# Where the decay powers of the first four chunks come from, and when those of the others are computed

## The chip, the cores and the metric

The kernel runs on one core of one Trainium2 chip. The metric is the device time of one execution in microseconds (us). The engines are TensorE (PE in the profile, its weight loads PEld), VectorE (DVE), ScalarE (ACT), GpSimd (POOL) and SyncE (SP), which issues the DMAs.

## What is computed

A recurrence over 768 steps, for 4 batches of 8 heads of size 40, and two gated feed-forward layers on its output:

```
for t in range(S):
    y[:, :, t] = einsum('bhd,bhde->bhe', r_t, state)
    Sa = einsum('bhde,bhe->bhd', state, a_t)
    state = state * w_t[:, :, None, :] - einsum('bhd,bhe->bhde', Sa, b_t)
    state = state + einsum('bhd,bhe->bhde', v_t, k_t)
x = y as 3072 rows of 320
x = (silu(x @ w_gate) * (x @ w_val)) @ w_out        # 320 -> 1536 -> 320
x = (sigmoid(x @ w_gate2) * (x @ w_val2)) @ w_out2
```

The decays `w` lie between 0.85 and 0.95. All is float32.

## The kernel before

The 768 steps are cut into 12 chunks of 64. Within a chunk the recurrence is linear algebra: every `a` row is multiplied by the running product of the decays up to its step (`p`), every `k` and `b` row ("keys", `tkb`) by the reciprocal product (`r`), and a triangular system of 64 unknowns per head is inverted. Only the state goes from chunk to chunk. So the chunks' states form a chain, and what is needed for a chunk beside the state can be made ahead.

**Stages.** Stage 1 (0 to 698 us) runs the 12 chunks. Each chunk is written as streams of steps, which `merge` interleaves by hand-given rates: `prep_a` of chunk m+2 (scaling of `a` and keys, transposes `tp` at L345, products `kps` at L407, and bn L416/L417, lq L419), `prep_b` of chunk m+1 (the inverse: `halves` for the chunks 0 to 2, `whole` for the later ones, with a trip through DRAM at L460 and L462; then `hps`, `zps`, `xps`), `chain` of chunk m (`qps`, `ups`, `sps` and the state update L658/L659, in two halves of the heads), `post` (L683, L691, L709, L719), and `extra`: layer 1 of chunk m-1's output for the 1536/128 = 12 blocks of weights that are loaded by then (`used[m]` blocks: 3 for the chunks 0 and 1, 5 next). One block for one chunk is a unit: 16 gate matmuls (`gv`, L929) and its output products (`po`, L947). Stage 2 (698 us to the end) runs as one stream of units what layer 1 has left, and layer 2; its gate matmuls are the tile `g`.

**Weight blocks.** `load_w` brings a block in three pieces. Each piece is one DMA into one of six buffers `raw` (L819), and then goes ScalarE L827, GpSimd L828, VectorE L831, L832, L836, L837, ScalarE L847, GpSimd L849 to L855. Blocks 0 to 2 are loaded beside chunk 0, blocks 3 and 4 in `extra(1)`.

**Powers before.** For chunk 0, `first()` makes `p` and `r` with ten scans each of 64 steps on VectorE (L127), and TensorE turns them into PSUM with 20 small matmuls each (L132; a float32 matmul stands as two records in the trace). For all other chunks `powers(n)` handles a group of four chunks at once, with the 32 heads of each chunk on 32 partitions: a load (L194), two clamps on VectorE (L201), and 28 products over 320 elements for `p` and `r` plus the reciprocal (L198, L217). For group 0 (chunks 1 to 3 are taken from it) most of them run on VectorE, right after chunk 0's scaling; for the groups 1 and 2 all run on GpSimd, beside the chunks 0 to 1 and 1 to 2. The results go to DRAM (`pd`, `rd`, L237) and come back in the layout the chunk needs (`pn` L327, `ld` L318, `pe` L351), and GpSimd multiplies with them (L365 for `a`, L369 for keys). `post` uses `pn` too.

**Order.** After `merge` the framework's scheduler orders each engine's queue. An engine runs its queue in order, and an instruction that waits holds what stands behind it. `behind` fixes one instruction after another on its engine.

## Time and profile before

| what | us |
|---|---|
| median of 3 runs | 1353.06 (1348.85 to 1354.39) |
| the profiled execution | 1346.3 |
| its span, first to last instruction | 1344.6 |
| TensorE busy in the span | 1242.4 (92%) |
| VectorE, ScalarE, GpSimd busy | 758.2, 595.3, 587.3 |

The profile gives the busy time of each engine over a stretch, the order of an engine's instructions in time with the idle time ahead of each and what ended it, and groups of instructions by line. The granted clock is that of TensorE as a share of full speed: 1.00 is 2.4 GHz, 0.5 is 1.2 GHz. The stretches below are cut where the second half of a chunk's state update (L659) ends, to within some us: chunk 0 at 97.1 us, chunk 1 at 171, chunk 2 at 235.6, and so on; from there, a later chunk takes 42 to 45 us in the steady part of stage 1.

### The profile page before, as it was taken

The numbers are of one execution on the slowest core, as the hardware profiler recorded it, in microseconds if no ns is written. First come the engines' busy times: TensorE is split into PE (matmuls) and PEld (weight loads), VectorE is DVE, ScalarE is ACT, GpSimd is POOL, SyncE is SP. The second block draws the span as 40 slices with busy tenths as digits, with TensorE's granted clock in tenths as the row PEclk, the third lists the DMA queues.
The fourth block names the chain that finished last, engine by engine and source line by source line (L and its number), as shares of the span: only waits on it lengthen the run. The fifth ranks groups of instructions, "written<-read, shape, count | busy, mean of one in ns | idle before, by whom it ended". The sixth has DMA issues, their size and how long they took to land.

```text
span 1344.6 us, 34131 instructions
## 1 busy us (share of the span) xinstructions
PE 1242.4 (92%) x13965; PEld 1178.6 (88%) x13965; DVE 758.2 (56%) x1575; ACT 595.3 (44%) x1439; POOL 587.3 (44%) x797
## 2 busy tenths in 40 slices
PE   4487988799999999989899999999999999999996
PEld 4376877698898988878898999999999999999996
DVE  8658676885676778686878888943111111111121
ACT  7464635446455655554443444423333333333331
POOL 5457375422232223345786788832222222222221
PEclk7566858699799999999999999999999999999998
DMA  8843738534424543353355554322000000000000
GB/s 227 202 123 92 157 101 179 132 109 123 127 64 122 142 115 77 84 137 110 108 169 170 185 174 153 100 93 68 22 23 22 22 23 23 23 23 22 11 12 14
DMA packets 164632, 130.44 MB, mean 97 GB/s; under 512 B 110832, under 2 KB 142576, under 8 KB 164080
## 3 DMA queue, kind: packets, MB, share of 16 engines
q1 hardware_dynamic: 164464, 128.15, 33.8%
q8 instruction: 112, 1.84, 0.6%
q14 instruction: 56, 0.46, 0.1%
...
## 4 chain that ended last, share of the span: by engine, by line
PE 68%; DVE 12%; DMA 6%; ACT 5%; POOL 4%; issue 4%; SPq 1%; POOLq 0%; ACTq 0%; DVEq 0%
PE g L929 28%; PE po L947 17%; PE gv L929 8%; PE kps L407 3%; PE tp L345 3%; PE yps L709 2%; PE aps L683 2%; DMA wt<-in_a_w_dram 2%; PE qps L619 1%; DMA xs<-ob 1%; PE ups L637 1%; DVE pr L447 1%; DVE ds L837 1%; POOL wp L198 1%; DMA ld<-rd 1%
## 5 line engine op out<-in xcount | busy, mean ns | idle before, releaser
L929 PE MATMUL g<-x,w 128*128 128x256 f32 x3552 | 491.1, 282 | 4.8 <-DVE g L935 2.6
L929 PEld LDWEIGHTS g<-x,w 128*128 128x128 f32 x3552 | 460.5, 189 | 7.0 <-DVE g L935 3.8
L938 POOL TENSOR_TENSOR hl<-g,hh 128x256 fp32r<-128x256 f32 x288 | 221.2, 769 | 460.1 <-ACT hh L937 422.6
L936 DVE TENSOR_TENSOR g<-g,g 128x256 f32<-128x256 f32 x222 | 93.8, 423 | 307.6 <-PE g L929 297.6
L937 ACT CAST hh<-g 128x256 fp32r<-128x256 f32 x288 | 117.0, 406 | 254.1 <-DVE g L936 231.5
L947 PE MATMUL po<-w,hh 128*128 128x320 f32 x1152 | 223.8, 311 | 1.0 <-ACT hh L937 0.6
L947 PEld LDWEIGHTS po<-w,hh 128*128 128x128 f32 x1152 | 175.3, 189 | 2.3 <-ACT hh L937 1.2
L929 PE MATMUL gv<-x,w 128*128 128x256 f32 x1056 | 154.6, 295 | 5.2 <-ACT x L881 2.4
L929 PEld LDWEIGHTS gv<-x,w 128*128 128x128 f32 x1056 | 137.1, 195 | 10.2 <-ACT x L881 3.9
L947 PE MATMUL po<-w,hl 128*128 128x320 f32 x576 | 141.6, 317 | 1.0 <-POOL hl L938 1.0
L933 ACT ACTIVATE g<-g 128x256 f32<-128x256 f32 x222 | 85.1, 383 | 126.3 <-PE g L929 114.9
L849 POOL TENSOR_TENSOR dt<-dt,w 128x384 f32<-128x384 f32 (+1 forms) x72 | 77.4, 1074 | 65.8 <-ACT w L847 29.6
L947 PEld LDWEIGHTS po<-w,hl 128*128 128x128 f32 x576 | 91.3, 189 | 2.7 <-POOL hl L938 1.5
L419 DVE TENSOR_TENSOR lq<-kps,part 64x256 f32<-64x256 f32 x96 | 40.4, 421 | 89.0 <-ACT bn L417 87.6
L407 PE MATMUL kps<-lq,kbt 104*128 104x128 f32 x384 | 72.1, 348 | 9.8 <-ACT kbt L403 6.0
L447 DVE TENSOR_TENSOR pr<-part,sn 128x4 f32<-128x4 f32 (+4 forms) x135 | 78.1, 578 | 2.8
L407 PEld LDWEIGHTS kps<-lq,kbt 104*128 104x128 f32 x384 | 63.8, 252 | 13.9 <-ACT kbt L403 7.6
L453 DVE TENSOR_REDUCE part<-pr 128x2 f32<-128x4 f32 (+4 forms) x135 | 66.7, 494 | 3.1
L847 ACT CAST w<-dt 128x384 fp32r<-128x384 f32 (+1 forms) x72 | 35.5, 495 | 64.0 <-DVE dt L832 57.0
L837 DVE SCALAR_TENSOR_TENSOR ds<-raw,ds 128x384 f32<-128x384 uint32 (+1 forms) x72 | 61.7, 857 | 1.0
L416 ACT ACTIVATE bn<-kps 32x256 f32<-32x256 f32 x96 | 35.9, 374 | 57.3 <-PE kps L407 35.3
L683 PE MATMUL aps<-rbd,ut 104*128 104x128 f32 x384 | 58.1, 296 | 2.6 <-DVE am L691 2.6
(156 smaller groups left out, 1772.3 us busy)
## 6 DMA issues: line engine op xcount, KB each, us to landing
...
```

The source lines that it names most:

```text
L407: nc.tensor.matmul(kps[:, n].rearrange("p h t -> p (h t)"), lhsT=kbt[0:PW, n, :], rhs=lq[m % 3][0:PW, 4 * g4 + n].rearrange("p h t -> p (h ...
L447: nc.vector.tensor_tensor(out=o, in0=xs[:, 0:kk, None, 0:n].to_broadcast([P, kk, 2, n]), in1=sn[:, None, n : n + 2, 0:n].to_broadcast([P, ...
L453: nc.vector.tensor_reduce(out=xs[:, 0:kk, n : n + 2], in_=o, axis=AX.X, op=ALU.add)
L683: nc.tensor.matmul(aps[:, n, h2], lhsT=ut[0:PW, x, 2 * h2 : 2 * h2 + 2].rearrange("p u s -> p (u s)"), rhs=rbd[0:PW, x, h2].rearrange("p b ...
L837: nc.vector.scalar_tensor_tensor(out=sg.bitcast(F32), in0=lo.bitcast(U32), scalar=2.0**-52, in1=sg.bitcast(F32), op0=ALU.mult, op1=ALU.mult,)
L849: sub(out=tf, in0=tf, in1=w.bitcast(F32), op=ALU.subtract)
L929: nc.tensor.matmul(gv[n], lhsT=p, rhs=q, start=e == 0, stop=e == len(seq) - 1)
L933: nc.scalar.activation(out=g, in_=gv[0], func=AF.Sigmoid)
L936: nc.vector.tensor_tensor(out=g, in0=gv[1], in1=g, op=ALU.mult)
L937: nc.scalar.copy(out=hh, in_=g)
L938: self.heng.tensor_tensor(out=hl, in0=g, in1=hh.bitcast(F32), op=ALU.subtract)
L947: self.nc.tensor.matmul(ops[u], lhsT=p[:, us], rhs=q, start=first and n == 0, stop=last and n == 2)
```

## The change

**Chunks 0 to 3** (`FS = 4`) take their powers from scans over whole rows: ten rows of 66 elements stand behind one another on each partition, and one scan of 660 elements does all (L138; the addend is a tile `one` that holds a 1 at the start of each row, and zeros under the row's data restart the product there). `r` runs backwards with the reciprocal of `p`'s end as its start. TensorE turns the results into PSUM with 20 + 20 matmuls `dtp` (L153; two halves each), VectorE multiplies `a` and keys straight from PSUM (L403, L410), and ScalarE copies `p` to `pn`, which goes once to DRAM (`pq`, L172) and is loaded again by `post` (L337). The ends of the chunk (`pend`) come from one product and one small matmul (L160, L166). Group 0's `powers` and its loads, stores, and GpSimd products (L365, L369) for the chunks 1 to 3 are gone.

**Groups 1 and 2** (`all_powers`) are emitted one after the other beside chunk 0, all on GpSimd; group 1's first clamp stands behind chunk 0's keys on VectorE. Each group still stores to `pd` and `rd`. The group-2 load goes into the buffer `wq` that group 1's stores read.

**Weights.** The blocks 3 and 4 are loaded in `extra(0)` (their buffers `wt` and `wq` are those of the groups' powers), so chunk 1's `extra` has 5 blocks instead of 3: two units of layer 1 move from stage 2 (222 to 220 units) to stage 1. Until `extra(0)`, `load_w` has two `raw` buffers instead of six, since the scans of the chunks 1 to 3 live in the other ones (`raw2` to `raw5`).

```
-        load = nc.sync.dma_start(out=q[rows, 0:C]..., in_=w[32 * ms[0] : ...])
-        if n == 1:
-            behind(load, "pn")
+        nc.sync.dma_start(out=q[rows, 0:C]..., in_=w[32 * ms[0] : ...])
...
-            if n == 1:
-                behind(clamp, ("state", 0))
+            behind(clamp, "keys")
...
+    def all_powers():
+        for n in range(1, len(groups)):
+            yield from powers(n)
...
+    def scan(o, x, js, way):
+        flat = lambda t: t[:, js].rearrange("p j t -> p (j t)")[:, ::way]
+        nc.vector.tensor_tensor_scan(
+            out=flat(o), data0=flat(x), data1=flat(one), initial=0.0, op0=ALU.mult, op1=ALU.add
+        )
...
+    def turn(to, x, half):
+        for b2, hs in enumerate(HALF):
+            sel = ident.rearrange(...)[:, :, b2] if half else ident
+            last = nc.tensor.matmul(to[hs], lhsT=x, rhs=sel, ...)
...
+    def scanned(m):
+        x, p, r = scan_tiles(m)
+        load_w0(m, x)
...
+        def by_p(ps, ds):
+            v = ps.rearrange("p (d n h) -> p n h d", n=8, h=2)
+            nc.vector.tensor_tensor(out=pairs(an)[..., ds], in0=heads(xa)[..., ds], in1=v, op=ALU.mult)
+            nc.scalar.copy(out=heads(pn)[..., ds], in_=v)
+        def by_r(ps, ds):
+            v = ps.rearrange("p (d n h) -> p n h d", n=16, h=2)
+            for q in range(2):
+                nc.vector.tensor_tensor(out=pairs(tkb[m % 3], sl)[..., ds], in0=heads(xk[q])[..., ds], in1=v[:, sl], op=ALU.mult)
+        scan_p(x, p)
...
+        scan(r, x, slice(0, 10), -1)
...
-    for _ in powers(0):
-        pass
...
-                todo.append((powers(1), *QP))
+                todo.append((all_powers(), *QP))
...
-                ffn = Ffn(nc, ident, (raws, x_p, h_p, ptp, [(pg, "gv")], po), True)
+                ffn = Ffn(nc, ident, (raws[:2], x_p, h_p, ptp, [(pg, "gv")], po), True)
...
+                if m == 0:
+                    ffn.raw = raws
...
-                for f in {-2: range(NFA - 2), 1: range(NFA - 2, NFA)}.get(m, ()):
+                for f in {-2: range(NFA - 2), 0: range(NFA - 2, NFA)}.get(m, ()):
```

How the queues change, at three places. In the rows, `out<-in` are the program's names; `part_...` are slices of shared buffers.

VectorE, about chunk 0's state updates (`sps` added at L658, decayed at L659), before; `am`, `sn` and `ysb` belong to `post` and to chunk 1's inverse, `wp` and `wq` are group 1's clamps:

```order
L691 TENSOR_TENSOR am<-aps,part_86 128x512 [waits PE_49]
L477 SCALAR_TENSOR_TENSOR sn<-sn,part_86 128x256 [waits Activation_49]
L658 TENSOR_TENSOR part_86<-sps,part_86 40x4x2x40 [waits PE_49]
L658 TENSOR_TENSOR part_86<-sps,part_86 40x4x2x40
L483 TENSOR_TENSOR sn<-sn 128x128 [waits DVE_49]
L659 TENSOR_TENSOR part_86<-part_86,pend 104x4x2x40 [waits DVE_49]
L201 TENSOR_SCALAR wp<-wq 128x2560 [waits DMAHW5_49,DMAHW6_49,DMAHW3_49,DMAHW0_49]
L484 TENSOR_TENSOR sn<-sn 128x8x16 [waits DVE_49,Activation_49]
L831 TENSOR_SCALAR dt<-dt 128x320 [waits Pool_49]
L201 TENSOR_SCALAR wq<-wq 128x2560 [waits DMAHW6_49,DMAHW5_49,DVE_49]
```

After (L716 and L717 are the state updates, L231 the clamps, now of group 2, L483 the products `lq` of chunk 1):

```order
L716 TENSOR_TENSOR part_86<-sps,part_86 40x4x2x40 [waits PE_49]
L716 TENSOR_TENSOR part_86<-sps,part_86 40x4x2x40
L483 TENSOR_TENSOR lq_210<-kps,part_86 64x4x64 [waits Activation_49]
L717 TENSOR_TENSOR part_86<-part_86,pend 104x4x2x40 [waits DVE_49]
L231 TENSOR_SCALAR wp<-wq 128x2560 [waits DMAHW5_49,DMAHW6_49,DMAHW4_49,DMAHW3_49]
L483 TENSOR_TENSOR lq_210<-kps,part_86 64x4x64 [waits PE_49,Activation_49]
L749 TENSOR_TENSOR am<-aps,part_86 128x512 [waits PE_49]
L878 TENSOR_SCALAR dt<-dt 128x384 [waits Pool_49]
L231 TENSOR_SCALAR wq<-wq 128x2560 [waits DMAHW3_49,DMAHW2_49,DMAHW4_49,DMAHW1_49,DVE_49]
L879 SCALAR_TENSOR_TENSOR dt<-raw,dt 128x384 [waits DMAHW5_49,DVE_49]
L483 TENSOR_TENSOR lq_210<-kps,part_86 64x4x64 [waits Activation_49]
L539 STREAM_TRANSPOSE sn<-bn 128x512
```

Before, the clamps of group 1 stand behind the second half of chunk 0's state; now those of group 2 stand behind its first half.

SyncE's queue ahead of the load of chunk 1's values (`v`, `part<-in_a_v`), before; `pn` and `ld` bring powers of chunk 1 or 2 from DRAM, `raw` are weights:

```order
L327 DMA pn<-pd 64x640 x2
L318 DMA ld<-rd 64x2x320 x2
L311 DMA ld<-in_a_a_dram 128x640
L819 DMA raw<-in_w_dram 128x640
L315 DMA ld<-in_a_kb_dram 128x640
L318 DMA ld<-rd 64x2x320 x2
L819 DMA raw<-in_w_dram 128x768 x2
L335 DMA part_203<-in_a_v_dram 64x640 x2
```

After (`pd` and `rd` are stores of group 1, `wq<-in_a_w` is the load of group 2):

```order
L866 DMA raw<-in_w_dram 128x768
L258 DMA pd<-wp 32x65x40 x4
L866 DMA raw<-in_w_dram 128x640
L866 DMA raw<-in_w_dram 128x768
L258 DMA rd<-wq 32x64x40 x4
L866 DMA raw<-in_w_dram 128x768
L226 DMA wq<-in_a_w_dram 128x2560
L866 DMA raw<-in_w_dram 128x640
L346 DMA part_197<-in_a_v_dram 64x640 x2
```

Two groups of four stores and the load of group 2 now stand ahead of the values, and the loads from `pd` and `rd` are gone.

TensorE in the inverse of chunk 1 (`hps`, `zps`, `xps`), up to chunk 1's first `ups`, before; the `kps` are chunk 2's, then chunk 3's:

```order
L524 MATMUL hps<-part_218,pr 16x16 x64
L345 MATMUL tp<-ident,part_88 104x128 x4
L354 MATMUL pep<-ident,part_86 104x16
L407 MATMUL kps<-lq_217,kbt 128x128 x4
L564 MATMUL zps<-x1t,bn 32x32 x32
L345 MATMUL tp<-ident,tkb_89 104x128 x8
L580 MATMUL xps<-part_218,zt 32x32 x32
L407 MATMUL kps<-lq_198,kbt 128x128 x4
L875 MATMUL xtp<-ident,ysb 128x128 x4
L637 MATMUL ups<-qs,part_218 64x40 x15
```

After (`dtp` are the turns of chunk 3's `p`, s_1606, and `r`, s_1607):

```order
L586 MATMUL hps<-part_212,pr 16x16 x64
L153 MATMUL dtp<-ident,s_1606 64x64 x13
L471 MATMUL kps<-lq_211,kbt 128x128 x4
L153 MATMUL dtp<-ident,s_1606 64x64 x3
L626 MATMUL zps<-x1t,bn 32x32 x32
L153 MATMUL dtp<-ident,s_1607 64x128 x15
L471 MATMUL kps<-lq_211,kbt 128x128 x4
L642 MATMUL xps<-part_212,zt 32x32 x32
L153 MATMUL dtp<-ident,s_1607 64x128 x5
L153 MATMUL dtp<-ident,s_1606 64x64 x4
L166 MATMUL dtp<-part_86 104x16
L695 MATMUL ups<-qs,part_212 64x40 x16
```

Chunk 3's 40 turns now stand between the products of chunk 1's inverse, ahead of its `ups`.

## Rows read from the trace of the kernel before

**Rows 1.** Stretches: start:end, length, then busy us (instructions) per engine, clock, DMA, GB/s

```profile
16.00:97.10 81.10, 51.10 (x772) 44.44 (x772) 52.23 (x109) 42.56 (x103) 41.80 (x55) 0.56 0.65 168
97.10:171.00 73.90, 62.82 (x1020) 55.21 (x1016) 54.00 (x94) 38.77 (x92) 43.43 (x52) 0.72 0.53 132
171.00:235.60 64.60, 54.66 (x835) 48.94 (x829) 44.52 (x82) 28.73 (x68) 46.48 (x57) 0.69 0.56 129
235.60:285.90 50.30, 42.49 (x592) 37.76 (x590) 41.29 (x90) 25.35 (x62) 18.05 (x25) 0.80 0.49 134
285.90:333.60 47.70, 45.77 (x672) 41.62 (x673) 31.74 (x65) 26.80 (x65) 11.92 (x16) 0.96 0.41 113
333.60:383.40 49.80, 47.92 (x659) 43.33 (x657) 31.42 (x64) 25.07 (x61) 11.69 (x16) 0.86 0.37 101
...
427.00:470.00 43.00, 43.00 (x654) 39.05 (x654) 33.52 (x74) 25.84 (x63) 12.61 (x17) 1.00 0.46 118
...
700.00:1344.00 644.00, 627.58 (x4952) 623.91 (x4950) 257.58 (x551) 223.89 (x572) 271.15 (x373) 0.99 0.20 64
```

**Rows 2.** VectorE by operation, 0 to 40 us: names, shapes, count | busy, mean ns | idle

```profile
L198 DVE TENSOR_TENSOR wp<-wp 128x320 f32<-128x320 f32 x14 | 10.7, 764 | 0.3
L198 DVE TENSOR_TENSOR wq<-wq 128x320 f32<-128x320 f32 x7 | 3.4, 483 | 0.1
...
L127 DVE TENSOR_TENSOR_SCAN r<-w,r,part 128x63 f32<-128x63 f32 x10 | 2.5, 324 | 0.0
L127 DVE TENSOR_TENSOR_SCAN p<-w,part 128x64 f32<-128x64 f32 x10 | 1.9, 270 | 0.0
...
L156 DVE TENSOR_TENSOR tkb<-tkb,f 128x320 f32<-128x320 f32 x4 | 1.7, 483 | 0.0
```

**Rows 3.** ScalarE in order of time, 36 to 97 us: start, us, operation [idle before]

```profile
58.54 0.54 ACT L827 ACTIVATE dt<-raw 128x384 f32<-128x384 f32 x1 [5.15 <-POOL w L853]
...
70.07 0.49 ACT L827 ACTIVATE dt<-raw 128x320 f32<-128x320 f32 x1 [3.04 <-POOL w L853]
...
80.84 0.55 ACT L827 ACTIVATE dt<-raw 128x384 f32<-128x384 f32 x1 [3.68 <-POOL w L855]
```

**Rows 4.** GpSimd by operation, 97 to 147 us

```profile
L198 POOL TENSOR_TENSOR wp<-wp 128x320 f32<-128x320 f32 x14 | 12.5, 894 | 0.4
```

**Rows 5.** SyncE's DMA queue in order of time, 0 to 260 us

```profile
150.54 7.23 SPq L237 DMA_DIRECT2D rd<-wq  x4
...
209.96 9.32 SPq L237 DMA_DIRECT2D rd<-wq  x4
...
221.51 2.08 SPq L460 DMA_DIRECT2D xd<-part  x2
```

**Rows 6.** VectorE in order of time, 36 to 210 us

```profile
85.92 0.47 DVE L659 TENSOR_TENSOR part<-part,pend 104x320 f32<-104x320 f32 x1
...
107.43 5.12 DVE L490 TENSOR_TENSOR pr<-x,sn 128x128 f32<-128x128 f32 x1
...
172.80 1.50 DVE L201 TENSOR_SCALAR wp<-wq 128x2560 f32<-128x2560 f32 x1 [1.84 <-DMA xs<-ob]
...
207.94 0.70 DVE L457 STREAM_TRANSPOSE x1t<-part 128x512 f32<-128x512 f32 x1
```

**Rows 7.** TensorE in order of time, 0 to 60 us and about 114 us

```profile
5.08 2.40 PE L132 MATMUL f<-ident,p 128*64 128x64 f32 x40 [5.08 <-DVE p L127]
7.26 3.52 PE L132 MATMUL f<-ident,r 128*64 128x128 f32 x40
...
114.10 1.94 PE L709 MATMUL yps<-part,rbd 104*64 104x40 f32 x32 [5.78 <-DVE am L691]
```

**Rows 8.** TensorE, the gate matmuls of stage 2: count, duration, first and last

```profile
L929 PE MATMUL g<-x,w x3552: 274/281/389, 698.1 to 1329.9; 128*128 128x256 f32 x198
```

**Rows 9.** VectorE by operation, 214 to 262 us

```profile
L837 DVE SCALAR_TENSOR_TENSOR ds<-raw,ds 128x384 f32<-128x384 uint32 (+1 forms) x5 | 3.8, 769 | 0.1
...
L832 DVE SCALAR_TENSOR_TENSOR dt<-raw,dt 128x384 int32<-128x384 int32 (+1 forms) x5 | 3.2, 644 | 0.0
```

More of the change, by code (lines that the diff above doesn't have):

```diff
@@ new lines, in scan_p @@
+    def scan_p(x, p):
+        for c in (0, C + 1):
+            nc.vector.memset(x[:, :, c : c + 1], 0.0)
+        xw = x[:, :, 1 : C + 1]
+        nc.vector.tensor_scalar(out=xw, in0=xw, scalar1=WLOW, scalar2=WHIGH, op0=ALU.max, op1=ALU.min)
+        scan(p, x, slice(0, 10), 1)
+        nc.vector.reciprocal(out=one[:, :, C + 1], in_=p[:, :, C])
+    def turn(to, x, half):
+        for b2, hs in enumerate(HALF):
+            sel = ident.rearrange("p (y b h) -> p y b h", b=2, h=2)[:, :, b2] if half else ident
+            last = nc.tensor.matmul(to[hs], lhsT=x, rhs=sel, start=True, stop=True, tile_position=(0, hs.start))
+        return last
@@ L375, in scaled @@
             yield
-    def prep_a(m):
-        if m:
+    def scanned(m):
+        x, p, r = scan_tiles(m)
+        load_w0(m, x)
+        new = lambda: wk.tile([P, NS * D], F32, tag="ld", name="ld", bufs=3)
+        xa, *xk = new(), new(), new()
+        nc.sync.dma_start(out=xa, in_=a[m])
+        for q in range(2):
+            nc.sync.dma_start(out=xk[q], in_=kb[m, q])
+        yield
+        heads = lambda x: x.rearrange("p (n h d) -> p n h d", h=2, d=D)
+        tp = lambda: ptp.tile([P, 4 * P], F32, tag="tp", name="dtp")
+        pn = wk.tile([P, 2 * H * D], F32, tag="pn", name="pn", bufs=2)
+        def by_p(ps, ds):
[4 more added lines that the diff above has]
+            v = ps.rearrange("p (d n h) -> p n h d", n=16, h=2)
+            for q in range(2):
+                sl = slice(8 * q, 8 * q + 8)
+                nc.vector.tensor_tensor(
+                    out=pairs(tkb[m % 3], sl)[..., ds], in0=heads(xk[q])[..., ds], in1=v[:, sl], op=ALU.mult
+                )
+        scan_p(x, p)
+        ps = tp()
+        for j in range(8):
+            turn(ps[:, 64 * j : 64 * j + 64], p[:, j, 0:C], True)
+        by_p(ps, slice(0, 32))
+        yield
+        scan(r, x, slice(0, 10), -1)
+        for k in range(3):
+            ps = tp()
+            js = range(4 * k, min(4 * k + 4, 10))
+            for i, j in enumerate(js):
+                turn(ps[:, P * i : P * i + P], r[:, j, 2:], False)
+            if k == 2:
+                for i in range(2):
+                    turn(ps[:, 256 + 64 * i : 320 + 64 * i], p[:, 8 + i, 0:C], True)
+                ends_scan(m, p, ps[:, 384:400])
+                by_p(ps[:, 256:384], slice(32, 40))
+                save_p(m, pn)
+            by_r(ps[:, 0 : P * len(js)], slice(16 * k, 16 * k + 4 * len(js)))
+            yield
+    def prep_a(m):
+        if 0 < m < FS:
+            yield from scanned(m)
+            if m == FS - 1:
+                done.add("scans")
+        elif m:
+            while m not in rd:
+                yield
             en = ends(m)
@@ L484, in halves @@
         nc.vector.tensor_tensor(out=od, in0=od, in1=nt, op=ALU.add)
-        if m == 0:
-            stores("zt", (2, 3))
         for kk in range(1, 8):
@@ L592, in prep_b @@
             nc.scalar.mul(out=X[lo, :, 32:64], in_=ps[lo], mul=-1.0)
-        if 0 < m < len(groups):
-            while ("w", m) not in done:
-                yield
-            stores("zt", groups[m])
         yield
@@ L729, in ahead @@
     def ahead(m):
-        n = m + 2
-        if n == 2 and n < len(groups):
-            while groups[n - 1][-1] not in rd:
-                yield
-            yield from powers(n)
         yield from extra(m - 1, out)
@@ L767, in attention @@
     nc.gpsimd.memset(tkb[2][..., D:64], 0.0)
-    for _ in powers(0):
-        pass
-    pends[0] = [x for x in ends(0)][1]
-    if NCH > 1:
-        for i in range(2):
-            store(1, i)
     start = [(prep_b(0), *QB)]
```

179 lines of the change are left out of this document (85 added, 94 removed).

## The prediction

> **What bounds the kernel now.** I read the stretches first, one per chunk of stage 1. From 700 us on, TensorE is busy 627.58 of 644 us [rows 1]: stage 2 gets shorter only if matmuls leave it. In stage 1 a steady chunk takes 43.00 us with TensorE busy throughout at granted clock 1.00. The early chunks are far from that: 81.10 us up to chunk 0's state (clock 0.56), then 73.90 (0.72), 64.60 (0.69), 50.30 (0.80), 47.70 (0.96) and 49.80 (0.86) [rows 1]. There TensorE is idle for 30.0, 11.1, 9.9, 7.8, 1.9 and 1.9 us (length less busy time), and much of its work runs at the lower of its two levels, 1.2 GHz, behind those gaps. So the early chunks are bound by a chain through all engines, and what it takes from or adds to that chain counts; the lower clock multiplies it.
>
> Who ends the gaps I read in order of time. In the head, ScalarE stands 5.15, 3.04 and 3.68 us before the first step of a weight piece (L827), each time until GpSimd frees a buffer [rows 3]; GpSimd in turn is held by loads of powers from DRAM. VectorE spends 10.7 and 3.4 us on group 0's products there [rows 2]. In chunk 1's part, TensorE waits 5.78 us for VectorE [rows 7], which stood in one product of 128 elements for 5.12 us [rows 6], while a product of 320 elements is done in 0.48 [rows 2]; GpSimd ran group 1's products back to back at that time.
>
> **The change part by part.** I sum against the profiled execution (1346.3 us, span 1344.6, 1.7 around it), which lies 6.8 us under the median of 1353.06; the difference is then taken off the median.
>
> *A, up to chunk 0's state (81.10 us).* Removed: the three waits of ScalarE, 5.15 + 3.04 + 3.68 = 11.9 us, since no load of powers from DRAM stands in GpSimd's queue any more. VectorE's 14.1 us of products go too, but I count them at nothing, because what takes their place is of like size. Added is the scaling of chunk 1 on VectorE. Scans took 1.9 and 2.5 us [rows 2] for ten rows; I take the same for one scan over all of them, as it goes over as many elements. Multiplying from PSUM costs 0.483 us for 320 elements [rows 2]: `a` (640 per partition) is two such, the keys (1280) four, 2.9 us. With a clamp and the ends that is 8.0 us a chunk, which I count in full, since it lies between the steps of chunk 0's inverse in VectorE's queue.
>
> A new wait comes on top. Group 2's clamp stands behind the first half of chunk 0's state on VectorE; `lq` and `am` and the second half of the state queue behind it. Its load must wait for group 1's stores. Before, from the first of the `rd` stores at 150.54 to the clamp at 172.80 it took 22.3 us [rows 5, 6]. GpSimd's 28 products at 0.894 us [rows 4] are 25.0 us; it has its weight pieces besides (41.80 us busy in 81.10 [rows 1], of which I put 23 ahead of the last product). From 16 us on that is 64 us for the stores, and 86.7 for the clamp, up to 94 if the pieces are held by only two buffers. The state's first half ended at 86.4 before [rows 6], and will at 82 to 84. So the wait is 4 to 10 us, and I take 7. A: -11.9 + 8.0 + 7 = **+3.1**. Below: the waits gone and everything else beside other work, -12. Above: wait of 10, scaling in full, one stall of 5.78 as in [rows 7], less 11.9, +12.
>
> *B, chunk 0 to 1 (73.90).* TensorE gets the turns of two chunks, 2.40 + 3.52 = 5.9 us each [rows 7], 11.8 in all; chunk 3's stand ahead of chunk 1's `ups`, on the path. Group 1's GpSimd products leave, and with them the 5.78 us stall: +6.0; I let 2 of it fall into the 11.1 us of idle time: **+4**. From 0 (the idle time takes them) to +12 (all on the path, the stall stays).
>
> *C, chunk 1 to 2 (64.60).* Group 2's products leave GpSimd (25 us) and its clamps leave VectorE. In come two units of layer 1 and the six pieces of the blocks 3 and 4, whose L837 and L832 alone are 0.769 + 0.644 = 1.4 us each [rows 9]. A unit in stage 2 costs (1329.9 - 698.1) / 222 = 2.85 us [rows 8], so two are 5.7. I take the steady 43.0 us, the 5.7, and of the 9.9 us idle what the two clamps of 1.5 [rows 6] don't explain, 6.9: 55.6, which is **-9**. Between -16 (no gap left) and +5 (the units come, nothing goes).
>
> *D, chunk 2 to 3 (50.30).* VectorE is busy 41.29 us here [rows 1]; five weight pieces leave it, 7.1 us for L837 and L832 [rows 9]. The stores on SyncE's queue that hold the trip of chunk 3's inverse through DRAM, from 208.6 (end of L457) to 221.51 [rows 5, 6], go as well. I take the level of 44: **-6**, between -8 and 0.
>
> *E, chunks 3 to 5 (47.70 and 49.80).* 11.5 us over the steady level, mostly clock; with the gap ahead closed I take **-3**, between -8 and +2.
>
> *F, stage 2.* 222 units become 220: **-5.7**, the one sure term.
>
> Single edits with one answer: the DRAM trip of `pn` for the chunks 0 to 3 is only read in `post`, tens of microseconds later, and costs nothing; GpSimd loses about 5 us a chunk of scaling and was not the one that ended last.
>
> Sum: 3.1 + 4 - 9 - 6 - 3 - 5.7 = -16.6; 1353.06 - 16.6 = 1336.5, so **1337**.
>
> One rule speaks against the change. [rows 6] shows VectorE in a product of two SBUF inputs for 5.12 us while GpSimd multiplies. The Trainium skill, "SBUF — State Buffer", section "Who interferes with whom", says that a VectorE instruction with two SBUF inputs and a GpSimd one that reads SBUF contend for one port pair, and that the later one is fully blocked. The row fits it; but in chunk 2's inverse the same products ran beside GpSimd's with little loss, so it doesn't hold for every overlap. By the rule the sum would go to the last rival below.
>
> **The rivals.**
> 1. *Much faster.* With the gaps closed TensorE stays at the 2.4 GHz level. In B its 62.82 us at 0.72 are 45.2 at full speed; with turns of 9.5 and the old idle time of 11.1 that is 66, -8; A 0, C -15, D -6, E -4, F -5.7: -38.7, **1314**. For it: the steady row at clock 1.00. Against it: the waits of the chain stay many and short.
> 2. *No change.* The work on TensorE sets the early stretches at the clock it gets: A +3, B 62.82 + 11.8 = 74.6 plus stalls, +7; C 54.66 + 5.7 with part of the idle time, -4; D -2; F -5.7: -1.7, **1351**. For it: TensorE is busy 85% of B and C. Against it: clock there.
> 3. *Slower, by the clamp of group 2.* If GpSimd's products take as long as the two-buffer weights let them, the load lands late; at a wait of 20 instead of 7 us A is 13 worse, and TensorE has nothing meanwhile, so B runs at A's 0.56 instead of 0.72: 45.2 / 0.56 - 62.82 = +18. -16.6 + 13 + 18 = +14, **1367**. It decides from a wait of about 12 us on (+5 + 18 - 16.6 = +6). For it: the 22.3 us from store to clamp. Against it: the head has 50 us for the products.
> 4. *Slower, by collisions.* Group 1's products now run beside chunk 0's inverse, group 2's beside chunk 1's. Each stall of 5.12 for about 0.3 costs 4.8; five of them are 24: +7.4, **1361**. From four on the gain is gone. For it: the one row. Against it: only one such row.
> That the change doesn't do what it says can be left out: the queues show it.
>
> **How the numbers follow.** A difference within 0.5% (6.8 us) can't be told from none here. Forecast 0.34, rival 1 0.12, rival 2 0.24, rival 3 0.19, rival 4 0.11. Faster: 0.34 + 0.12 = 0.46; same 0.24; slower 0.19 + 0.11 = 0.30. The range goes from just below rival 1 to just above rival 3, 1310 to 1370; the ends of all terms at once (-50 and +25) lie further out and are left to the remaining 2 in 10.
>
> **What would show it.** After: chunk 0's state at about 100 us, with one gap ahead of group 2's clamp of 4 to 10 us on VectorE (rival 3: 20 and more; A right if ScalarE's waits are gone); B at 78 us with the turns between `hps` and `ups`; C near 55 and D near 44 with clock over 0.8 (rival 2: 60 and 48); stage 2 shorter by 5.7. Products of VectorE that take over 3 us beside GpSimd speak for rival 4. The forecast is wrong if the clock in B to D doesn't rise, since C, D and E rest on it.

## The result and the profile after

The changed kernel takes 1337.3 us (median of 6 runs, 1336.07 to 1343.62) against 1353.01 before (1347.31 to 1354.39). The ratio of the runs (not that of the two medians) is 0.9903, with a 95% interval from 0.9875 to 0.9931: 1.0% faster, 9 to 17 us. The forecast was 1337. The profiled execution took 1336.4 us (span 1334.6); that of before took 1346.3, 6.8 under its median, so the two traces show only 10 of the 16 us.

The stretches of the changed kernel, cut again where the second half of a chunk's state update ends (as [rows 1]; columns: stretch, length, busy us of TensorE, its weight loads, VectorE, ScalarE, GpSimd, then the granted clock, DMA share and GB/s):

```profile
16.00:102.90 86.90, 56.45 (x932) 49.80 (x932) 58.80 (x105) 43.72 (x103) 60.04 (x74) 0.63 0.54 128
102.90:184.30 81.40, 66.19 (x961) 58.46 (x962) 55.80 (x122) 44.85 (x105) 40.96 (x52) 0.73 0.64 150
184.30:244.20 59.90, 55.24 (x936) 50.41 (x935) 43.80 (x88) 28.34 (x69) 15.37 (x20) 0.77 0.38 108
244.20:284.00 39.80, 38.94 (x650) 35.10 (x649) 32.41 (x69) 24.48 (x60) 10.70 (x15) 1.00 0.48 123
284.00:329.80 45.80, 43.05 (x666) 39.00 (x665) 32.13 (x70) 25.56 (x62) 11.62 (x16) 1.00 0.43 112
329.80:375.30 45.50, 44.78 (x710) 40.63 (x709) 32.54 (x70) 25.46 (x62) 12.59 (x16) 1.00 0.45 119
```

Clock and idle time show where it went. Up to chunk 0's state it takes 102.9 us instead of 97.1, from there to chunk 1's 81.4 instead of 73.9, with the clock no better (0.73 against 0.72). Chunk 2's state then comes 60.0 us later (64.3 before), chunk 3's 39.8 (51.7 before), at clock 1.00 instead of 0.80 and with 0.9 us of idle time on TensorE instead of 7.8. So the head lost 13 us, and the two chunks behind it won 16.

Stage 2 has 220 units (as [rows 8]; 3520 / 16):

```profile
L976 PE MATMUL g<-x,w x3520: 274/281/583, 693.7 to 1319.4; 128*128 128x256 f32 x196
```

VectorE in the changed kernel, about chunk 0's state (as [rows 6]; start, us, operation, and in brackets the idle time ahead and what ended it):

```profile
10.49 1.53 DVE L138 TENSOR_TENSOR_SCAN s<-s,one 128x660 f32<-128x660 f32 x1
...
82.71 0.48 DVE L717 TENSOR_TENSOR part<-part,pend 104x320 f32<-104x320 f32 x1
89.79 1.49 DVE L231 TENSOR_SCALAR wp<-wq 128x2560 f32<-128x2560 f32 x1 [6.60 <-DMA wq<-in_a_w_dram]
...
101.72 1.14 DVE L717 TENSOR_TENSOR part<-part,pend 104x320 f32<-104x320 f32 x1
```

The scan of 660 elements takes 1.53 us, less than the ten short ones of before (1.9, [rows 2]). The first half of chunk 0's state ends at 83.2 us, and then VectorE waits 6.60 us for group 2's load (L231). The second half ends at 102.9, 19.7 us after the first; before, these were 10.7 us apart.

TensorE, the waits that matter (as [rows 7]):

```profile
18.82 1.95 PE L356 MATMUL tp<-ident,part 128*104 128x128 f32 x8 [6.27 <-ACT pend L168]
...
92.52 2.08 PE L741 MATMUL aps<-rbd,ut 104*128 104x128 f32 x8 [4.79 <-DVE am L749]
...
106.83 2.04 PE L741 MATMUL aps<-rbd,ut 104*128 104x128 f32 x8 [5.33 <-DVE x L558]
```

The first transposes wait for ScalarE to read chunk 0's ends from PSUM. With the clamp's wait come two stalls of 4.79 and 5.33 us, both for VectorE: the first begins while the clamp waits, the second lies at chunk 0's state.

SyncE's queue (as [rows 5]):

```profile
72.22 6.81 SPq L258 DMA_DIRECT2D rd<-wq  x4
...
84.22 0.35 SPq L226 DMA_DIRECT2D wq<-in_a_w_dram  x1
...
231.78 1.32 SPq L524 DMA_DIRECT2D xd<-part  x2
```

Group 1's second stores are issued from 72.22 us, group 2's load at 84.22; the load is there at 89.8. The trip of chunk 3's inverse through DRAM starts at 231.78 with no stores ahead of it, and still 10.9 us after VectorE's last step for it (220.91): the profile names a ScalarE copy (L670) as what it waited for.

ScalarE ahead of the first step of a weight piece (as [rows 3]):

```profile
54.88 0.55 ACT L874 ACTIVATE dt<-raw 128x384 f32<-128x384 f32 x1 [3.37 <-POOL w L902]
...
63.04 0.55 ACT L874 ACTIVATE dt<-raw 128x384 f32<-128x384 f32 x1 [2.86 <-POOL w L900]
```

Of the waits for GpSimd (5.15, 3.04 and 3.68 us before), 3.37 and 2.86 are left, now with group 1's products between GpSimd's steps of the pieces.

### The profile page after: what moved, and what is told of

Same layout as the page of the kernel before. It is cut to its first block, busy times and chain, and to the rows that moved or that the text cites. A ratio compares the mean times of both kernels' runs of the same rounds, so it can differ in the third digit from the quotient of the medians.

```text
span 1334.6 us, 34566 instructions
## 1 busy us (share of the span) xinstructions
PE 1239.4 (93%) x14209; PEld 1179.4 (88%) x14209; DVE 754.5 (57%) x1578; ACT 599.3 (45%) x1446; POOL 563.1 (42%) x767
## 4 chain that ended last, share of the span: by engine, by line
PE 75%; DVE 12%; issue 3%; ACT 3%; DMA 2%; POOL 2%; SPq 1%; POOLq 0%; DVEq 0%; ACTq 0%
PE g L976 30%; PE po L994 18%; PE gv L976 9%; PE tp L356 3%; PE kps L471 3%; PE aps L741 2%; PE yps L767 2%; PE qps L677 1%; PE ups L695 1%; SPq L258 1%; DVE dt L879 1%; DVE pr L511 1%; DVE part L517 1%; PE zps L626 1%; PE xps L642 1%
## 5 line engine op out<-in xcount | busy, mean ns | idle before, releaser
L976 PE MATMUL gv<-x,w 128*128 128x256 f32 x1088 | 160.0, 296 | 5.9 <-ACT x L928 3.6
L976 PEld LDWEIGHTS gv<-x,w 128*128 128x128 f32 x1088 | 142.0, 197 | 11.9 <-ACT x L928 6.0
L483 DVE TENSOR_TENSOR lq<-kps,part 64x256 f32<-64x256 f32 x96 | 40.4, 421 | 86.5 <-ACT bn L481 82.8
L511 DVE TENSOR_TENSOR pr<-part,sn 128x4 f32<-128x4 f32 (+4 forms) x135 | 74.2, 550 | 2.9
L471 PE MATMUL kps<-lq,kbt 104*128 104x128 f32 x384 | 64.4, 320 | 3.4 <-ACT kbt L467 1.8
L356 PE MATMUL tp<-ident,part 128*104 128x128 f32 x288 | 50.0, 301 | 16.2 <-ACT pend L168 6.3
L741 PEld LDWEIGHTS aps<-rbd,ut 104*128 104x128 f32 x384 | 51.3, 203 | 15.6 <-issue 8.6
L471 PEld LDWEIGHTS kps<-lq,kbt 104*128 104x128 f32 x384 | 56.6, 226 | 7.2 <-issue 3.7
```

Of the source, the lines that this page charges most:

```text
L356: t = nc.tensor.transpose(ps[0 : x.shape[1], n, :], x, ident)
L471: nc.tensor.matmul(kps[:, n].rearrange("p h t -> p (h t)"), lhsT=kbt[0:PW, n, :], rhs=lq[m % 3][0:PW, 4 * g4 + n].rearrange("p h t -> p (h ...
L511: nc.vector.tensor_tensor(out=o, in0=xs[:, 0:kk, None, 0:n].to_broadcast([P, kk, 2, n]), in1=sn[:, None, n : n + 2, 0:n].to_broadcast([P, ...
L741: nc.tensor.matmul(aps[:, n, h2], lhsT=ut[0:PW, x, 2 * h2 : 2 * h2 + 2].rearrange("p u s -> p (u s)"), rhs=rbd[0:PW, x, h2].rearrange("p b ...
L976: nc.tensor.matmul(gv[n], lhsT=p, rhs=q, start=e == 0, stop=e == len(seq) - 1)
```

## The experiments

Nearly all of them change the time through the first four chunks. For each kernel the table gives the median, the ratio to the kernel before, run beside it (with medians from 1349.6 to 1353.0), with its interval, the end of chunk 3's state in its profile, and the rest of the span behind that. A kernel's own runs differ by up to 16 us, and the rest, in which none of the experiments but the second changes the work, took 1043 to 1062 us; so a stage is read from the trace, and the median says what is left of it. Stage 2 took 640 to 645 us of that rest in every one of these traces (646.5 in the kernel before); what differs is the later chunks of stage 1 (400 to 417 us).

| kernel | median us | ratio (95%) | chunk 3's state | rest |
|---|---|---|---|---|
| before | 1353.0 | 1 | 286.9 | 1057.7 |
| changed | 1337.3 | 0.9903 (0.9875 to 0.9931) | 284.0 | 1050.6 |
| 1 clamp behind the whole state | 1322.1 | 0.9797 (0.9779 to 0.9815) | 269.9 | 1048.3 |
| 2 weights at the old place | 1341.4 | 0.9934 (0.9909 to 0.9958) | 285.0 | 1051.1 |
| 3 scans held | 1345.3 | 0.9956 (0.9936 to 0.9975) | 284.3 | 1062.4 |
| 4 chunk 0's copies on VectorE | 1321.1 | 0.9788 (0.9768 to 0.9808) | 272.2 | 1043.7 |
| 5 turns twice | 1329.4 | 0.9842 (0.9809 to 0.9875) | 283.8 | 1044.2 |
| 6 no products | 1326.0 | 0.9812 (0.9779 to 0.9846) | 276.0 | 1048.8 |
| 7 stores ahead of the trip | 1349.6 | 0.9998 (0.9963 to 1.0034) | 293.9 | 1054.9 |
| 8 first and fourth together | 1337.3 | 0.9905 (0.9871 to 0.9940) | 283.0 | 1051.1 |
| 9 group 2 behind chunk 1's inverse | 1319.8 | 0.9787 (0.9755 to 0.9819) | 263.2 | 1054.6 |
| 10 ninth and fourth together | 1339.2 | 0.9916 (0.9886 to 0.9946) | 277.5 | 1055.7 |
| 11 eighth without group 2's products | 1323.0 | 0.9817 (0.9784 to 0.9850) | 275.9 | 1042.9 |
| 12 ninth with turns twice | 1325.9 | 0.9818 (0.9799 to 0.9838) | 273.4 | 1055.5 |

### 1. Group 2's clamp behind the whole of chunk 0's state

```
     def all_powers():
         for n in range(1, len(groups)):
+            while n == 2 and "state0" not in marks:
+                yield
             yield from powers(n)
...
-            behind(clamp, "keys")
+            behind(clamp, "state0" if n == 2 else "keys")
```

(`state0` is the second half's update L717 of chunk 0.)

> Edit: group 2's load, clamps and products are written behind chunk 0's chain, and its first clamp stands on VectorE behind the second half of chunk 0's state instead of the first. In the changed kernel VectorE waited 6.60 us for group 2's load between the two halves, and the second half ended at 102.9 us (97.1 in the kernel before). Theory (the clamp's wait is on the path and is paid in full): the second half ends at 93 to 96 us and the median falls by 6 to 9 us under the changed kernel's 1337.3, to 1328 to 1331. Rival (it is given back): group 2's products and stores come later, chunk 1's part grows by as much, and the median stays within 3 us of 1337.

Measured: 1322.1, 15 us under the changed kernel. VectorE, the second half of the state and the clamp:

```profile
92.55 1.03 DVE L719 TENSOR_TENSOR part<-part,pend 104x320 f32<-104x320 f32 x1
93.50 1.48 DVE L231 TENSOR_SCALAR wp<-wq 128x2560 f32<-128x2560 f32 x1
```

The clamp doesn't wait any more: the load lands while VectorE works on the chain. The stretches up to chunk 0's state and on to chunk 1's:

```profile
16.00:93.60 77.60, 50.56 (x899) 44.70 (x901) 53.39 (x104) 43.47 (x103) 52.98 (x67) 0.67 0.60 144
93.60:167.60 74.00, 63.09 (x1006) 55.76 (x1003) 56.26 (x118) 42.54 (x100) 47.12 (x55) 0.82 0.60 157
```

93.6 instead of 102.9 us, as the theory has it; but the next stretch falls too, from 81.4 to 74.0, with clock 0.82 instead of 0.73, and the two stalls of TensorE (4.79 and 5.33) are gone. The wait was paid twice: once where it stood and once more in the chunk behind it. The edit also starts group 2's products on GpSimd later (at 97.52 instead of 91.37 us), so that the second part is due to the wait alone isn't shown.

### 2. Blocks 3 and 4 loaded at the old place

```
-                for f in {-2: range(NFA - 2), 0: range(NFA - 2, NFA)}.get(m, ()):
+                for f in {-2: range(NFA - 2), 1: range(NFA - 2, NFA)}.get(m, ()):
```

> Edit: the weight blocks 3 and 4 are loaded beside chunk 2 again, as in the kernel before; all else is the changed kernel. Stage 2 has 222 units again. Theory (term F: two units leave stage 2, and chunk 1 to 2 pays for them; chunk 2 to 3 got short because the stores of powers no longer hold the DRAM trip of chunk 3's inverse, and the clock is up): stage 2 is 5.7 us longer, chunk 1 to 2 some 5 shorter than 59.9, chunk 2 to 3 stays under 44; median 1337 to 1342. Rival (chunk 2 to 3 fell from 51.6 to 39.8 us because the weight pieces left VectorE): it goes back to 47 to 51 and the median to 1345 to 1350.

Measured: 1341.4, 4 us above the changed kernel, within the theory's range; the intervals of the two overlap, so those 4 us are not clear of the noise. Its stretches for chunk 1 to 2 and 2 to 3:

```profile
185.50:243.60 58.10, 53.44 (x960) 48.36 (x958) 42.31 (x85) 27.82 (x68) 15.25 (x21) 0.74 0.40 114
243.60:285.10 41.50, 37.87 (x617) 34.45 (x616) 32.40 (x68) 24.11 (x59) 9.15 (x12) 0.96 0.44 121
```

Two units more remain for stage 2, chunk 1 to 2 is only 1.8 us shorter, not 5, and the stretch of chunk 2 to 3 stays at 41.5 us, at clock 0.96. So moving the blocks is worth about 4 us, within the noise. That VectorE's weight pieces made that stretch long before is not tested by it: in this run none of their VectorE steps lies in it, and three pieces' lie in the one ahead.

### 3. Scans of chunks 2 and 3 held behind the inverses

```
+        marks[("turned", m)] = <second STREAM_TRANSPOSE of halves(m)>
...
-        scan(p, x, slice(0, 10), 1)
+        behind(scan(p, x, slice(0, 10), 1), ("turned", m - 2))
```

> Edit: the scans of chunk 2 are held on VectorE behind the last turn (STREAM_TRANSPOSE) of chunk 0's inverse, those of chunk 3 behind that of chunk 1's inverse. In the changed kernel chunk 2's clamp, two scans, reciprocal and ends (1.14 + 1.52 + 1.78 + 0.21 + 0.45 = 5.1 us) stand among the steps of chunk 0's inverse, long before they are needed. Theory (the scaling is on the path of chunk 0's inverse, as term A counts it): the first state update comes 3 to 5 us earlier than 83.2 us and the median falls by 3 to 6 us, to 1331 to 1334. Rival (VectorE has room there, or group 2's load is then what all wait for): the state's second half stays at 101 to 103 us and the median within 3 us of 1337.

Measured: 1345.3, 8 us slower: neither theory nor rival. TensorE's first product of chunk 0's inverse does start earlier, at 51.12 us instead of 55.51:

```profile
51.12 1.91 PE L573 MATMUL hps<-x1t,bn 16*32 16x16 f32 x128 [7.10 <-DVE x1t L563]
```

but VectorE then has the scans' work where chunk 0's chain needs it:

```profile
87.79 1.49 DVE L231 TENSOR_SCALAR wp<-wq 128x2560 f32<-128x2560 f32 x1 [0.78 <-DMA wq<-in_a_w_dram]
89.20 2.04 DVE L717 TENSOR_TENSOR part<-part,pend 104x320 f32<-104x320 f32 x1
...
116.81 3.74 DVE L138 TENSOR_TENSOR_SCAN s<-s,one 128x660 f32<-128x660 f32 x1
```

The clamp of group 2 now stands ahead of the first half's last step (L717), which ends at 91.2 us instead of 83.2, and a scan beside GpSimd's products takes 3.74 us. The 4.4 us are there and are given back within 40 us. Another 12 us lie in the rest of the program (1062.4), where nothing was changed: 8 of them in the later chunks of stage 1 (417.4 us against 409.7, clock 0.97 against 0.99). That part has no cause shown, and the profiled execution, 1348.4, was the slowest of the twelve.

### 4. Chunk 0's copies from PSUM on VectorE

```
-            nc.scalar.copy(out=heads(pn), in_=pnv)
+            copy(heads(pn), pnv)      # VectorE, tensor_scalar times 1.0
...
-            ends_scan(0, p, pt)
+            ends_scan(0, p, pt, copy)
```

> Edit: chunk 0's copies of p and of its ends from PSUM are made by VectorE instead of ScalarE, where they stood behind 16 us of fills and held TensorE's first transposes to 18.82 us (16.36 in the kernel before) until ScalarE had read the banks. Theory (those copies delay the head): the first transposes start near 15 us, and chunk 0's state and the median come 1 to 2.5 us earlier. Rival (ScalarE's next step, the copy of the transposes, waits for the same fills until 18 us): TensorE starts earlier, but the state and the median stay within 1 us.

Measured: 1321.1, 16 us faster, some ten times what was expected, and not for that reason. TensorE's transposes start at 16.49 instead of 18.82 us, yet the first half of the state ends 2.7 us later, at 85.9. VectorE there:

```profile
85.44 0.48 DVE L718 TENSOR_TENSOR part<-part,pend 104x320 f32<-104x320 f32 x1
86.45 1.67 DVE L232 TENSOR_SCALAR wp<-wq 128x2560 f32<-128x2560 f32 x1 [0.54 <-DMA wq<-in_a_w_dram]
```

Group 1's products were done earlier, group 2's load was issued at 79.93 instead of 84.22 us, and the state came later: the clamp waits 0.54 us instead of 6.60. By accident it takes away the same wait as the first experiment, and chunk 0 to 1 falls from 81.4 to 70.5 us.

### 5. The turns twice

```
-        for b2, hs in enumerate(HALF):
+        for b2, hs in (2 if <dtp> else 1) * list(enumerate(HALF)):
```

> Edit: every turn of the chunks 1 to 3 (dtp) is issued twice; all else is the changed kernel. 40 matmul records of p took 2.40 us and 40 of r 3.52 us in chunk 0, so TensorE gets 5.9 us more for each of three chunks. Theory (term B: about half of the turns of the chunks 2 and 3 lies on the path, chunk 1's falls into waits for VectorE and ScalarE): 5 to 9 us more, the median at 1342 to 1346. Rival a (the turns lie in TensorE's idle time): within 3 us of 1337. Rival b (all on the path): 15 or more, 1352.

Measured: 1329.4, 8 us faster with more work: all three expectations missed. The clamp waits here too, now between the two steps of the state's first half:

```profile
87.91 1.49 DVE L231 TENSOR_SCALAR wp<-wq 128x2560 f32<-128x2560 f32 x1 [6.52 <-DMA wq<-in_a_w_dram]
89.32 0.49 DVE L717 TENSOR_TENSOR part<-part,pend 104x320 f32<-104x320 f32 x1
```

Chunk 3's state comes at 283.8 us, as in the changed kernel, and 6.4 us of the gain lie in the rest of the program, for which no cause was found. With that wait inside, the run can't give a price of the turns; the twelfth tries it without the wait.

### 6. No products on GpSimd

```
-        mult = lambda x, y: nc.gpsimd.tensor_tensor(out=x, in0=x, in1=y, op=ALU.mult)
+        mult = lambda x, y: None
```

> Edit: the 28 + 1 products of each of the groups 1 and 2 are not made (the powers of the chunks 4 to 11 are left out, so the output differs); loads, clamps and stores stay. GpSimd has 52 us less to do, and group 1's stores and group 2's load come far before chunk 0's state. Theory (the products cost only through the late load of group 2, the 6.6 us wait and what follows it): the same gain as with the clamp behind the whole state (1322), so 1318 to 1325. Rival (VectorE and GpSimd also collide over the whole of the chunks 0 and 1): VectorE's products in the inverses get shorter, and the median falls below 1312.

Measured: 1326.0, just above the theory's 1318 to 1325 and far from the rival's 1312. VectorE's products in the two inverses, 40 to 130 us, in the changed kernel (count | busy us, mean ns):

```profile
L552 DVE TENSOR_TENSOR pr<-x,sn 128x8 f32<-128x8 f32 (+6 forms) x14 | 8.3, 590 | 0.3
```

and without GpSimd's products:

```profile
L552 DVE TENSOR_TENSOR pr<-x,sn 128x8 f32<-128x8 f32 (+6 forms) x14 | 4.6, 326 | 0.3
```

Each product takes 326 ns instead of 590, so GpSimd does slow VectorE there, by 3.7 us over both inverses; but all of GpSimd's products together cost no more in this run than the late clamp alone (11 against 15 us). It is no clean price: the first half of chunk 0's state ends at 88.2 us there instead of 83.2.

### 7. The stores back ahead of chunk 3's DRAM trip

```
+        if m == 3:
+            for i in range(8):
+                to = <DRAM tile of 65 x 32 x 40>
+                nc.sync.dma_start(out=to, in_=<x1t, repeated>)
         xd = dr.tile([4, NS, 16, 2, 32], F32, name="xd", tag="xd")
```

> Edit: eight stores of the size of a group's (32 x 65 x 40) into unused DRAM are put on SyncE's queue ahead of the DRAM trip of chunk 3's inverse, where the kernel before had group 2's stores (they held the trip from 208.6 to 221.5 us). In the changed kernel that trip is issued 10 us after its data are there, and chunk 2 to 3 takes 39.8 us (51.7 in the kernel before). Theory (the hold was what made chunk 2 to 3 long): it takes 46 to 52 us again, the median is 6 to 12 us higher, 1343 to 1349. Rival (the clock and VectorE's weight pieces did): under 43, and the median within 3 us of 1337.

Measured: 1349.6, 12 us slower, just above the theory's range; but chunk 2 to 3 takes 43.6 us, not the 46 to 52 of the theory. SyncE's queue:

```profile
222.82 17.08 SPq L526 DMA_DIRECT2D hold<-x1t  x8
240.00 3.46 SPq L529 DMA_DIRECT2D xd<-part  x2
```

The stores took 17.08 us to issue and held the trip, whose data were there at 222.8, to 240.0 us (231.78 in the changed kernel). Chunk 3's state comes 9.9 us later (293.9). Chunk 2 to 3 itself grew by 3.8 us only, the chunk ahead by 5 and the one behind by 5: the whole queue was held, not the trip alone. So what such stores cost at this place is shown, and that they made chunk 2 to 3 long is not.

### 8. The first and the fourth together

> Edit: both of the first and the fourth experiment (group 2's clamps behind the whole state of chunk 0; chunk 0's copies from PSUM on VectorE). The first gained 15 us and the fourth 16, and in both traces the 6.6 us wait of VectorE for group 2's load is gone, with the two stalls of TensorE behind it (4.79 and 5.33 us). Theory (both take away the same wait): 1318 to 1323, no sum. Rival (two separate gains): 1304 to 1310.

Measured: 1337.3. Neither: all of the gain was gone. The second half of chunk 0's state ends at 95.7 us, but chunk 0 to 1 takes 93.7. VectorE there:

```profile
106.23 12.17 DVE L138 TENSOR_TENSOR_SCAN s<-s,one 128x660 f32<-128x660 f32 x1
```

A scan that takes 1.53 us elsewhere took 12.17. GpSimd at that time:

```profile
106.38 0.85 POOL L229 TENSOR_TENSOR wp<-wp 128x320 f32<-128x320 f32 x1
...
115.34 0.85 POOL L229 TENSOR_TENSOR wq<-wq 128x320 f32<-128x320 f32 x1
116.15 2.89 POOL L229 TENSOR_TENSOR wp<-wp 128x320 f32<-128x320 f32 x2
```

GpSimd ran group 2's products, with two of a weight piece among them, one behind the other from 106.38 to 119.04 us, with no gap, and VectorE got through when that run was nearly over, at 118.40. TensorE stood still meanwhile:

```profile
103.53 1.14 PE L746 MATMUL aps<-rbd,ut 104*128 104x128 f32 x8
119.39 1.10 PE L359 MATMUL tp<-ident,part 128*104 128x128 f32 x4 [14.72 <-DVE part L406]
```

It waited 14.72 us. The 5.12 us of before ([rows 6]) look the same: that product started at 107.43 and ended at 112.55. GpSimd in the kernel before, the first and the last operation of its run and what came next:

```profile
107.47 0.85 POOL L849 TENSOR_TENSOR dt<-dt,w 128x320 f32<-128x320 f32 x1
...
111.55 0.85 POOL L198 TENSOR_TENSOR wq<-wq 128x320 f32<-128x320 f32 x1
117.82 1.68 POOL L369 TENSOR_TENSOR tkb<-ld 128x320 f32<-128x320 f32 x2 [5.42 <-PE yps L709]
```

The run went from 107.47 to 112.40 us.

### 11. The same without group 2's products

```
-        mult = lambda x, y: nc.gpsimd.tensor_tensor(out=x, in0=x, in1=y, op=ALU.mult)
+        mult = lambda x, y: nc.gpsimd.tensor_tensor(...) if n == 1 else None
```

> Edit: the kernel with both the first and the fourth change, and group 2's products are not made (the powers of the chunks 8 to 11 are left out, so the output differs). With both changes the median was 1337, no better than the changed kernel, and one scan of 660 elements on VectorE in chunk 1's inverse took 12.17 us (1.5 elsewhere), just while GpSimd made group 2's products with no gap between them. Theory (the scan stood still for GpSimd's products): it takes 1.5 to 2.5 us, chunk 0 to 1 falls from 93.7 to 70 to 78 us, and the median to 1312 to 1322. Rival (the order of the queues did it): chunk 0 to 1 stays over 85 us and the median over 1330.

Measured: 1323.0, just above the theory's range. The two scans of that chunk:

```profile
107.19 1.52 DVE L138 TENSOR_TENSOR_SCAN s<-s,one 128x660 f32<-128x660 f32 x1
...
110.94 1.52 DVE L138 TENSOR_TENSOR_SCAN s<-s,one 128x660 f32<-128x660 f32 x1
```

1.52 us each; chunk 0 to 1 takes 76.0 us instead of 93.7. GpSimd's products were what held the scan.

### 9 and 10. Group 2 behind chunk 1's inverse, alone and with the fourth

```
     def all_powers():
-        for n in range(1, len(groups)):
-            yield from powers(n)
+        yield from powers(1)
...
     def ahead(m):
+        if m == 0:
+            while "turned1" not in marks:
+                yield
+            yield from powers(2)
...
-            behind(clamp, "keys")
+            behind(clamp, "turned1" if n == 2 else "keys")
```

> Edit: group 2's load, clamps and products are written behind the VectorE part of chunk 1's inverse (they are needed from chunk 8 on), so that neither VectorE's wait for the load nor GpSimd's products of group 2 fall beside chunk 0's chain or chunk 1's inverse. Theory (wait and collisions with those products are what the chunks 0 and 1 lose): the second half of chunk 0's state ends near 94 us as in the first experiment, no VectorE instruction of chunk 1's inverse takes over 2 us longer than its like elsewhere, chunk 0 to 1 takes 68 to 74 us; median 1312 to 1320. Rival (it comes back in chunk 1 to 2, where the products and stores now stand, or the weight blocks 3 and 4 come late): chunk 1 to 2 over 64 us, median 1325 or more.

> Edit: the same, and chunk 0's copies from PSUM on VectorE as in the fourth experiment. Theory: with the wait gone otherwise, the copies on VectorE are worth only their own 1 to 2 us: within 3 us of the kernel without them. Rival (the fourth experiment's gain was that of the head): 10 us or more under it.

Measured: the ninth 1319.8, with the tenth at 1339.2. The ninth's stretches, up to the states of the chunks 0, 1, 2 and 3:

```profile
16.00:93.20 77.20, 53.04 (x893) 46.75 (x895) 52.75 (x104) 43.44 (x103) 52.80 (x66) 0.62 0.58 141
93.20:161.30 68.10, 58.96 (x989) 51.79 (x984) 54.78 (x117) 40.88 (x95) 41.06 (x52) 0.82 0.66 158
161.30:223.50 62.20, 56.63 (x959) 51.70 (x958) 46.88 (x96) 32.03 (x78) 21.48 (x29) 0.78 0.43 123
223.50:263.20 39.70, 39.47 (x642) 35.42 (x641) 31.30 (x66) 24.63 (x60) 11.45 (x15) 1.00 0.48 129
```

It is the fastest chain of all (chunk 3's state at 263.2 us, 23.7 earlier than before) and, with the first and the fourth experiment, the fastest kernel, 2.1% under the kernel before and 1.2% under the change. Chunk 0's state, chunk 0 to 1 and the median come as the theory has them; chunk 1 to 2 keeps to 62.2 us, and no step of chunk 1's inverse is held.

The tenth fits neither expectation. ScalarE there, in chunk 1's part:

```profile
146.89 0.51 ACT L900 CAST w<-dt 128x384 fp32r<-128x384 f32 x1 [6.50 <-DMA pd<-wp]
```

TensorE at the same time:

```profile
149.29 1.07 PE L356 MATMUL tp<-ident,part 128*104 128x128 f32 x4 [7.35 <-ACT part L702]
```

The cast of a weight piece into the buffer `wt` (L900) waited 6.50 us on ScalarE until group 2's store had read that buffer, the copies of the chain stood behind it, and TensorE waited 7.35 us. It is again one early instruction that waits for a transfer ahead of the chain's own steps. Chunk 3's state comes 14.3 us later than in the ninth; 4 of these lie ahead of chunk 0's state already, which this wait can't explain.

### 12. The ninth with the turns twice

> Edit: the kernel with group 2 behind chunk 1's inverse (1319.8, chunk 0 to 1 in 68.1 us), and every turn of the chunks 1 to 3 issued twice, 5.9 us more of TensorE's work for each chunk. There group 2's load no longer falls beside chunk 0, which made the first run with doubled turns hard to read. Theory after the runs so far (the turns lie in idle time of TensorE; the +4 of term B was not theirs): chunk 0 to 1 up by 0 to 4 us, the median within 4 us of 1320. Rival (as term B counts them, half of the turns or more on the path): chunk 0 to 1 at 74 to 80 us, the median at 1326 to 1334.

Measured: 1325.9, 6 us over the ninth. Chunk 0 to 1:

```profile
92.30:174.70 82.40, 67.39 (x1177) 60.08 (x1173) 56.12 (x119) 43.02 (x99) 44.83 (x54) 0.86 0.56 142
```

82.4 us instead of 68.1, with TensorE busy 8.4 us longer at much the same clock. The turns themselves take 16.53 us of TensorE in that stretch instead of 8.91, so 7.6 were added, less than the 11.8 that the price of chunk 0's turns gives for two chunks. The other 5.9 of the 14.3 us are idle time, 3.5 of them in one stall:

```profile
125.05 1.92 PE L627 MATMUL zps<-x1t,bn 32*32 32x32 f32 x64 [4.50 <-DVE x1t L605]
```

In the ninth run this wait is 1.03 us. VectorE had stood in a weight step (L883, 0.36 us elsewhere) for 3.68 us beside GpSimd's products of group 2. So TensorE's added time was not hidden, but what the turns cost by themselves is not separated from that collision. The profiled execution was the slowest of the five, and the intervals of the two ratios overlap, so the 6 us are a rough figure. The theory formed after the fifth run (idle time hides the turns) falls: its 0 to 4 us for the stretch are far exceeded.

## Why the prediction came out right, and which of its steps did not

In us, by the ends of the states in the two traces:

| term | predicted | measured |
|---|---|---|
| A, to chunk 0's state | +3.1 | +5.8 |
| B, chunk 0 to 1 | +4 | +7.5 |
| C, chunk 1 to 2 | -9 | -4.3 |
| D, chunk 2 to 3 | -6 | -11.9 |
| E, chunks 3 to 5 | -3 | -5.0 |
| the later chunks | 0 | +2.6 |
| F, behind the last state | -5.7 | -4.8 |
| sum | -16.6 | -10.1 (medians: -15.7) |

**A: the sizes hold, the price of the wait doesn't.** The wait of group 2's clamp was put at 4 to 10 us, 7 taken, and is 6.60. Its parts were off both ways: group 1's second stores began at 72.2 us, not 64, and from there to the clamp it took 17.6 us, not 22.3. The 22.3 us that it was taken from held another wait: for that clamp the profile names the store `xs` (the row at 172.80, [rows 6]). And 64 + 22.3 is 86.3, not 86.7. Without the wait the head is worth -3.5 and -3.9 us (93.6 and 93.2 in the first and ninth experiment), as -11.9 + 8.0 says. But that agreement is luck in its parts: ScalarE kept two of its waits, and only part of the scaling lay among the steps of chunk 0's inverse.

**B is the step that failed.** It was put at +4 and is +7.5, because it left out what the wait does to the chunk behind it: TensorE's stall of 5.33 us lies in B, and without the wait B is 74.0 us instead of 81.4 (first experiment), and 68.1 where group 2's products come later as well (ninth). The runs agree: with a wait of 6.5 to 7.8 us B is 81 to 84 us (changed kernel, second, seventh, and the fifth with its doubled turns), without it 68 to 79 (first, fourth, sixth, ninth, tenth, eleventh); the third has the clamp at another place, and the eighth and twelfth a collision. The wait priced at 7 cost 15 us of the median (first). The turns, which B was made of, were counted at 5.9 us a chunk; the second set takes 7.6 us for two chunks (twelfth). B let 2 of 11.8 us be hidden, and whether that share is right is open. The group-1 stall of 5.78 that it took off is gone.

**C and D share one gain.** C + D was put at -15 and is -16.2; D alone, at -11.9, is twice its term. D named two reasons, VectorE's weight pieces and the stores that hold the trip of chunk 3's inverse. The traces speak against the second: the trip is issued 13.7 us ahead of chunk 2's state in the kernel before (221.51) and 12.5 us ahead of it in the changed one (231.78), so it comes no earlier for the chain, and stores put back lengthen that stretch by 3.8 us only (seventh). The pieces did leave it. VectorE in chunk 2 to 3 of the kernel before (as [rows 9], but 235.6 to 285.9 us; count | busy us, mean ns | idle):

```profile
L837 DVE SCALAR_TENSOR_TENSOR ds<-raw,ds 128x384 f32<-128x384 uint32 (+1 forms) x4 | 3.3, 837 | 0.0
L832 DVE SCALAR_TENSOR_TENSOR dt<-raw,dt 128x384 int32<-128x384 int32 (+1 forms) x4 | 2.7, 686 | 0.0
L831 DVE TENSOR_SCALAR dt<-dt 128x384 int32<-128x384 int32 (+1 forms) x4 | 1.7, 422 | 1.5 <-POOL dt L828 1.5
L836 DVE TENSOR_SCALAR ds<-dt 128x384 int32<-128x384 int32 (+1 forms) x4 | 1.7, 416 | 0.1
```

Four pieces (not five) take 9.4 us of VectorE there, between the steps of chunk 4's inverse, and none of them is left in the changed kernel, where VectorE is busy 32.41 us instead of 41.29. Why they came so late before can be read at one place: ScalarE's cast of a piece (L847) waited 4.99 us, until 215.2, for group 2's store to have read the buffer that both use. So the powers' stores probably cost the kernel before through the pieces and not through the trip; that is read from the traces, and no run tests it. The clock rose from 0.69 and 0.80 to 0.77 and 1.00, as the forecast needed.

**E and F** hold: stage 2, from its first gate matmul, is 5.6 us shorter (640.9 against 646.5). Of the median the two blocks are worth about 4 us, within the noise (second).

**The sum.** That the median meets the forecast within 1 us is luck: by the traces A, B and the later chunks are 8.8 us worse than predicted and C to F 2.3 better, which leaves -10.1; the rest of the median's -15.7 is mostly that the profiled execution of the kernel before ran 6.8 us under its median.

**The rivals.** The third (slower by the clamp) has the right mechanism: its wait decided more than any term, but at 6.6 us it stayed under the 12 from which it turns the sign. The fourth (collisions) is real, but this kernel met little of it: the worst that VectorE met beside GpSimd was a step of a weight piece that took 2.17 us (0.49 elsewhere), while the eighth experiment had one 10.6 us longer and lost a gain of 15 us to it. The first (TensorE stays at the 2.4 GHz level) came half true, from chunk 2's state on.

What stays open is the rest of the program, behind chunk 3's state: with the same work it took 1043 to 1062 us in the traces, and the medians of the third and fifth experiment can't be put down to their edits alone. The difference lies in the chunks 4 to 11, not in stage 2.
